# Loading three half batches of q and k in another way: a plain load turned on TensorE, and two transposes from long source rows

## The chip, the cores and the metric
The kernel runs on one core of one Trainium2 chip. The metric is the device time of the whole program in microseconds (us). The core has five instruction streams that run side by side and meet at semaphores: TensorE (PE in the profile, its weight loads as PEld), VectorE (DVE), ScalarE (ACT), GpSimd (POOL) and SyncE (SP, which here only issues DMA transfers). Each engine works through its own list strictly in order.

## The reference
Eight batches, eight heads, 576 tokens, head dimension 64, all in float32. The computation is causal attention with a decay, followed by a feed-forward block with a short convolution and a gate:

```python
scores = scale * np.matmul(q, k.transpose(0, 1, 3, 2))
cum = np.cumsum(np.log(np.clip(f, 0.0001, 1.0)), axis=-1)
scores = np.where(causal, -1e9, scores + cum[:, :, :, None] - cum[:, :, None, :])
attn = softmax(scores)                       # over the last axis
x = (attn @ v), heads side by side           # 8 x 576 x 512
h = np.maximum(x @ w_in, 0.0)                # 512 -> 1024
conv_out[:, s] = sum(conv_w[k] * h[:, s + k - 1] for k in range(3))
out = (h / (1 + np.exp(-conv_out))) @ w_out  # 1024 -> 512
```

## The kernel before, in words
**Half batches.** Attention is done in 16 half batches of four heads (hb 0 to 15). For each, q and k arrive as two tiles of 128 partitions by 2,304 columns (four heads times 576 tokens). A float32 number is read as two 16-bit halves, so the 64 numbers of a token are 128 halves, one for each partition: the upper half of each number is its bfloat16 value and lies on an odd partition, the lower half on an even one. The transfer itself turns tokens into columns (`dma_start_transpose`, line 199). Even partitions are then of no use as numbers. For hb 0 to 5 an operation on VectorE multiplies them by zero and puts constants on three of them (`clamp`, line 205; tasks cl0 to cl5), after which two small transfers from DRAM (`rows_of`, lines 220 and 221; tasks rw1 to rw5) write the decay into some of these rows, so that one matmul gives score plus decay. From hb 6 on, two transfers do all of this (`fill`). hb 0 takes its decay through two additional matmuls and needs no rows from DRAM.

**Tasks.** For one half batch: q and k loads (tasks q*hb*.0 and q*hb*.1, for q and k), cleaning, decay rows, scores on TensorE in six groups (sd: blocks on the diagonal of two heads, so: the other blocks of one head, st: the tail of 64 tokens; line 319, with a mask matmul at line 327), the exponentials on ScalarE (ed, eo, et; lines 360, 377, 339), the product with v (pv, line 395), the division by the row sum on VectorE (n, lines 402 and 403), a turn back on TensorE (t, line 411) and its copy (tx, line 416). The feed-forward part of a batch is eight times f (line 425), r (ScalarE, line 435), c and d (VectorE, lines 440 and 442), a (ScalarE, line 459), g (VectorE, line 463), then o (line 470), its eviction e (line 480) and the store s.

**Order.** Nothing is scheduled by a planner. The string `ORDER` names all tasks in one sequence, and each engine gets its tasks in that sequence. A task that waits therefore holds back all that comes after it on its engine, SyncE's queue of transfers among them. The string begins as follows; the part from `q3.1` on is the second place that the change concerns:

```
cw cl0.0 q2.1 cl2.1 cl0.1 q1.0 cl1.0 q1.1 cl1.1 sd0 ed0 so0.0 eo0.0 ...
f0.4 r0.1 q3.1 d0.0 h0 r0.2 r0.3 cl3.1 c0.2 a0.0 r0.4 c0.3 d0.3 sd4 ... q3.0 eo4.0 a0.3 st2 q5.1 q5.0
f0.5 eo4.1 v1.0 cl3.0 rw3 g0.0 ... so5.1 eo5.1 g0.3 wo0 f0.7 r0.7 cl5.1
cl5.0 rw5 sd7 ed7 ...
```

The four transfers of hb 0 come before this, straight in the code. sd7 is the second pair of heads of hb 3 and is its first score task, so it is the one that meets the wait for rw3; in the same way sd2 is the first of hb 1.

**Storage.** q and k of four half batches lie in a ring of four tiles (qk0 to qk3), so hb 5 uses the tile of hb 1. PSUM is four tiles (ps0 to ps3), handed from task to task in the order of the string. hg0 and hg1 hold the gated values of two batches; hg1 is free until the second batch's feed-forward starts. Before, the rows of the convolution's weights lie in hg1 at the start and two constant rows in hg0.

Of the kernel before, what the change touches and what calls it, by code (L numbers as in the profile page):

```python
# [18 lines left out]
eo1.1 ki@POOL v0.0 v0.1 st0 rw1 v0.2 sd2 so2.0 v0.3 va0.0 cwt so2.1 v0.4 va0.1 et0 sd3 ed2 eo2.1 ed3 so3.0 eo2.0 pv0.0  # L19
n0.0 rw2 pv0.1 eo3.0 n0.1 so3.1 eo3.1 va1.0 va1.1 sd5 ed5 st1 et1 pv0.2 n0.2 wi0 wic0@POOL wi1 wic1@POOL pv1.0 n1.0  # L20
pv1.1 n1.1 pv1.2 n1.2 zc t0 so5.0 tx0@ACT eo5.0 wi3 wi2 wic3@ACT t1 tx1@DVE f0.0 f0.1 f0.2 f0.3 r0.0 wic2@ACT c0.0
f0.4 r0.1 q3.1 d0.0 h0 r0.2 r0.3 cl3.1 c0.2 a0.0 r0.4 c0.3 d0.3 sd4 so4.1 so4.0 ed4 d0.2 q3.0 eo4.0 a0.3 st2 q5.1 q5.0
f0.5 eo4.1 v1.0 cl3.0 rw3 g0.0 f0.6 r0.5 v1.1 a0.2 et2 c0.4 d0.4 v1.2 v1.3 a0.4 so5.1 eo5.1 g0.3 wo0 f0.7 r0.7 cl5.1
cl5.0 rw5 sd7 ed7 c0.1 g0.4 wo1 so7.1 eo7.1 c0.7 sd6 so6.1 eo6.1 g0.2 v1.4 so6.0 r0.6 va3.0 st3 et3 ed6 q4.1 c0.5 d0.5
so7.0 eo7.0 eo6.0 a0.5 c0.6 sd10 ed10 d0.1 q4.0 sd11 ed11 pv3.0 pv3.1 d0.7 va3.1 pv3.2 n3.0 va2.0 n3.1 n3.2 pv2.0
va2.1 wo2 woc0@ACT n2.0 a0.1 pv2.1 n2.1 pv2.2 a0.7 n2.2 so10.1 eo10.1 woc1@POOL v2.0 v2.3 t3 t2 tx2@ACT so10.0 eo10.0
# [43 lines left out]
class Plan:  # L70
# [34 lines left out]
def kernel(  # L105
# [11 lines left out]
    nc = tc.nc  # L117
# [37 lines left out]
    one1 = cpool.tile([128, 1], FP32, name="one1")  # L155
    lim = cpool.tile([128, 4], FP32, name="lim")
    mask = cpool.tile([128, 128], BF16, name="mask")
    taps = cpool.tile([128, NFF, 3, 128], FP16, name="taps")
    lit = cpool.tile([128, 6], FP32, name="lit")
    lii = cpool.tile([128, 3], I32, name="lii")  # L160
    hix = cpool.tile([128, 128], I32, name="hix")
# [20 lines left out]
    ps_t = [psum.tile([128, 1024], FP32, name=f"ps{t}") for t in range(4)]  # L182

    fsb, cum = u_t[0], u_t[1]
    cwrow = hg_t[1].rearrange("p f s -> p (f s)").bitcast(FP32)[0:3, 0:D_FF]

    plan = Plan({"ps": 4, "p": NP, "pt": NPT, "va": NVA, "vf": NVF, "xm": NX, "rc": NRC, "xt": NXT, "ht": NHT, "u": NU,
                 "hg": NHG, "ob": NOB, "pd": NPD, "p3": NP3})
# [3 lines left out]
    def ps_of(name):  # L192
        return ps_t[slot[name, "ps"]]


    def load_qk(hb, h0, nh, side):
        t, src = ((stq_t, q), (stk_t, k))[side]
        t = t[hb % RING]
        nc.sync.dma_start_transpose(  # L199
            t.bitcast(U16)[:, h0 * S:(h0 + nh) * S],  # L200
            src[hb // 2, HH * (hb % 2) + h0:HH * (hb % 2) + h0 + nh].bitcast(U16).rearrange("h s d2 -> (h s) d2"))

    def clamp(hb, h0, nh, side):
        t = (stq_t, stk_t)[side][hb % RING].bitcast(U16)[:, h0 * S:(h0 + nh) * S]
        nc.vector.tensor_scalar(t, t, lim[:, 2 * side:2 * side + 1], lim[:, 2 * side + 1:2 * side + 2],  # L205
                                op0=ALU.mult, op1=ALU.add)
# [52 lines left out]
    for side in range(2):  # L259
        nc.vector.tensor_copy(lim[:, 2 * side:2 * side + 1], lit[:, 1:2])  # L260
    nc.vector.tensor_scalar(sel_k, hfx[:, 0:4], lit[:, 2:3], None, op0=ALU.is_equal)
    nc.vector.tensor_scalar(ident, hfx, lit[:, 0:1], None, op0=ALU.is_equal)
    nc.vector.tensor_scalar(mask, hfx, lit[:, 0:1], -1e30, op0=ALU.is_lt, op1=ALU.mult)
    nc.vector.tensor_scalar(sel_q, hfx[:, 0:4].unsqueeze(2).broadcast_to((128, 4, 128)), lit[:, 0:1], -1.0,
                            op0=ALU.is_equal, op1=ALU.mult)
    nc.vector.tensor_scalar(one3, hfx[0:3, 0:3], lit[0:3, 0:1], None, op0=ALU.is_equal)

    plus, minus = (hg_t[0].bitcast(BF16)[0:BH, x, :] for x in range(2))
    nc.gpsimd.memset(plus, 1.0)
    nc.gpsimd.memset(minus, -1.0)  # L270
    nc.gpsimd.memset(zero, 0.0)
# [156 lines left out]
    def ht_of(b, ff):  # L428
        return ht_t[slot[f"r{b}.{ff}", "ht"]]
# [11 lines left out]
        else:  # L441
            nc.vector.scalar_tensor_tensor(u, ht[:, 2:2 + S], cwt[:, ff, 1:2], u, op0=ALU.mult, op1=ALU.add)  # L442

    def tap_weights(ff):
        for x in range(3):
            nc.gpsimd.tensor_scalar(taps[:, ff, x, :], ident, cw[:, ff, x:x + 1], None, op0=ALU.mult)

    def conv_pe(b, ff):
        ps, ht = ps_of(f"k{b}.{ff}"), ht_of(b, ff)
        for x in range(3):  # L450
            for a in range(2):
                nc.tensor.matmul(ps[:, MB + 288 * a:MB + 288 * (a + 1)], taps[:, ff, x, :],
                                 ht[:, x + 288 * a:x + 288 * (a + 1)], start=(x == 0), stop=(x == 2))

    def tanh(b, ff):
        if (b, ff) in CONV_PE:
            nc.scalar.activation(hg_of(b, ff), ps_of(f"k{b}.{ff}")[:, MB:MB + S], AF.Tanh)
# [62 lines left out]
    for hb in range(NHB):  # L520
        b = hb // 2
        was = hb - RING
        old = [f"st{was}"] + [f"sd{2 * was + y}" for y in range(2)] + [
            f"so{2 * was + y}.{s}" for y in range(2) for s in range(2)] if was >= 0 else []
        if hb == 0:
            for p in range(2):
                add(f"cl0.{p}", "DVE", [], lambda p=p: [clamp(0, 2 * p, 2, side) for side in (1, 0)])
            ready = [["cl0.0"], ["cl0.1"]]
        else:
            for side in range(2):  # L530
                add(f"q{hb}.{side}", "SP", old, lambda hb=hb, side=side: load_qk(hb, 0, 4, side))
            if hb < NCL:
                for side in range(2):
                    add(f"cl{hb}.{side}", "DVE", [f"q{hb}.{side}"], lambda hb=hb, side=side: clamp(hb, 0, 4, side))
                add(f"rw{hb}", "SP", [f"cl{hb}.{side}" for side in range(2)] + ["ki"], lambda hb=hb: rows_of(hb))
                ready = [[f"rw{hb}"]] * 2
            else:
                add(f"fi{hb}", "SP", [f"q{hb}.0", f"q{hb}.1", "zc", "ki"], lambda hb=hb: fill(hb))
                ready = [[f"fi{hb}"]] * 2
        if hb % 2 == 0:  # L540
            for kb in range(NKB):
                add(f"v{b}.{kb}", "SP", [], lambda b=b, kb=kb: load_v(b, kb), take=["vf"] if kb == 0 else [],
                    behind=[f"v{b}.0"] if kb else [])
# [102 lines left out]
```

## Time and profile before
| | |
|---|---|
| two runs | 261.69 and 263.29 us, median 262.49 |
| span of the profiled execution | 262.6 us |
| TensorE busy | 236.1 us, 90% |
| VectorE busy | 213.2 us, 81% |
| ScalarE busy | 207.1 us, 79% |
| GpSimd busy | 64.4 us, 25% |
| cleaning on VectorE, 128x2304 | 10 times, 876 ns each |
| issue of a transposing transfer on SyncE, min / median / max | 1.34 / 2.8 to 3.0 / 5.43 us, 34 in all |

The span is that of one profiled execution; beyond it the runs give only the whole time, and the median lies 0.1 us below the span. The profile names work by engine and source line. An idle time in front of an instruction is put down to what released it: `[2.59 <-DMA qk<-image]` says that the engine stood still for 2.59 us and that a transfer from the decay image into a q/k tile ended the wait. SPq is SyncE's own queue: its rows are the time in which it issued a transfer, not the transfer's own time. The granted clock of TensorE is listed by stretch; 0.50 is half speed.

### The profile page before, as it was taken

The numbers are of one execution on the slowest core, as the hardware profiler recorded it, in microseconds if no ns is written. First come the engines' busy times: TensorE is split into PE (matmuls) and PEld (weight loads), VectorE is DVE, ScalarE is ACT, GpSimd is POOL, SyncE is SP. The second block draws the span as 40 slices with busy tenths as digits, with TensorE's granted clock in tenths as the row PEclk, the third lists the DMA queues.
The fourth block names the chain that finished last, engine by engine and source line by source line (L and its number), as shares of the span: only waits on it lengthen the run. The fifth ranks groups of instructions, "written<-read, shape, count | busy, mean of one in ns | idle before, by whom it ended". The sixth has DMA issues, their size and how long they took to land.

```text
span 262.6 us, 6608 instructions
## 1 busy us (share of the span) xinstructions
PE 236.1 (90%) x2712; PEld 170.2 (65%) x2712; DVE 213.2 (81%) x342; ACT 207.1 (79%) x275; POOL 64.4 (25%) x104
## 2 busy tenths in 40 slices
PE   2495999578869999999999999999999999999991
PEld 1373787357645866778665788579758876766450
DVE  6553166987957999998997979999899999999940
ACT  3163669979887998996798999898999889696732
POOL 8400550014031104017003272027104641100000
PEclk9998599999979999999999999999999999999998
DMA  6999999999799999999999889998999901012225
GB/s 140 210 237 178 273 183 192 205 284 173 191 226 211 210 195 221 228 252 194 205 233 237 218 191 198 286 249 158 219 247 204 300 5 60 25 41 79 82 100 181
DMA packets 123328, 49.37 MB, mean 188 GB/s; under 512 B 113346, under 2 KB 114370, under 8 KB 123298
## 3 DMA queue, kind: packets, MB, share of 16 engines
q1 hardware_dynamic: 122908, 48.07, 86.1%
q0 software_dynamic: 304, 0.73, 1.0%
q8 instruction: 21, 0.34, 0.6%
q10 hardware_dynamic: 86, 0.16, 0.3%
q14 instruction: 9, 0.07, 0.1%
HBM read 19.91 MB, written 10.17 MB: 115 GB/s over the span
## 4 chain that ended last, share of the span: by engine, by line
PE 67%; SPq 10%; DVE 9%; ACT 7%; DMA 3%; issue 2%; ACTq 0%; DVEq 0%
PE ps L425 20%; PE ps L470 18%; PE ps L319 14%; PE ps L395 8%; SPq L199 8%; DMA qk<-image 3%; ACT pp L377 3%; PE ps L474 3%; DVE hg L463 3%; DVE xm L403 2%; PE ps L411 2%; PE ps L327 2%; ACT pp L360 1%; ACT hg L459 1%; DVE u L442 1%
## 5 line engine op out<-in xcount | busy, mean ns | idle before, releaser
L319 PE MATMUL ps<-qk 128*128 128x128 bf16 (+2 forms) x576 | 67.2, 249 | 13.5 <-DMA qk<-image 7.2
L425 PE MATMUL ps<-xt,w_in_f 128*128 128x288 f16 x512 | 69.5, 288 | 1.4 <-ACT xt L416 1.0
L377 ACT ACTIVATE pp<-ps 128x1024 f16<-128x1024 f32 x64 | 64.2, 1028 | 5.2 <-PE ps L319 3.5
L319 PEld LDWEIGHTS <-qk 128*128 128x128 bf16 x576 | 42.9, 102 | 31.9 <-DVE u L440 5.6
L440 DVE SCALAR_TENSOR_TENSOR u<-ht,cwt 128x576 f32<-128x576 f16 x64 | 54.4, 858 | 6.8 <-ACT ht L435 6.8
L425 PEld LDWEIGHTS <-w_in_f 128*128 128x128 f16 x512 | 49.3, 98 | 16.0 <-issue 2.8
L470 PE MATMUL ps<-w_out_f,hg 128*128 128x512 f16 x256 | 59.4, 379 | 0.0
L442 DVE SCALAR_TENSOR_TENSOR u<-ht,cwt,u 128x576 f32<-128x576 f16 x64 | 53.4, 845 | 1.7
L463 DVE SCALAR_TENSOR_TENSOR hg<-hg,ht 128x576 f16<-128x576 f16 x64 | 51.0, 820 | 2.6 <-ACT hg L459 2.6
L459 ACT ACTIVATE hg<-u,cw 128x576 f16<-128x576 f32 x64 | 48.9, 782 | 3.9 <-DVE u L442 3.7
L435 ACT ACTIVATE ht<-ps 128x576 f16<-128x576 f32 x64 | 40.8, 658 | 8.8 <-PE ps L425 7.4
L470 PEld LDWEIGHTS <-hg 128*128 128x128 f16 x256 | 24.4, 98 | 25.4 <-issue 0.4
L395 PE MATMUL ps<-va,pp 128*128 128x65 f16 x896 | 34.2, 193 | 0.8 <-ACT pp L377 0.4
L395 PEld LDWEIGHTS <-pp 128*128 128x128 f16 x896 | 32.5, 98 | 2.0 <-ACT pp L377 0.5
L234 POOL CAST va<-vf 128x1024 f16<-128x1024 f32 x16 | 17.6, 1105 | 63.9 <-DMA vf<-in_v_dram 50.8
L403 DVE TENSOR_TENSOR xm<-ps,rc 128x512 f16<-128x512 f32 (+1 forms) x48 | 28.9, 602 | 1.7
L363 POOL TENSOR_SCALAR_AFFINE_SELECT pp<-pd 128x1024 f16<-128x1024 f32 x16 | 19.6, 1230 | 43.3 <-ACT pd L360 43.3
L360 ACT ACTIVATE pp<-ps 128x1024 f16<-128x1024 f32 x16 | 16.3, 1027 | 15.3 <-PE ps L319 8.8
L480 ACT COPY ob<-ps 128x1024 f32<-128x1024 f32 (+1 forms) x20 | 16.5, 824 | 7.3 <-issue 5.0
L402 DVE RECIPROCAL rc<-ps 128x8 f32<-128x8 f32 (+1 forms) x48 | 9.3, 194 | 11.6 <-PE ps L395 10.6
L205 DVE TENSOR_SCALAR qk<-qk,lim 128x2304 uint16<-128x2304 uint16 (+1 forms) x14 | 10.6, 790 | 9.0 <-DMA qk<-in_k_dram 5.8
L360 ACT ACTIVATE pd<-ps 128x1024 f32<-128x1024 f32 x16 | 16.2, 1029 | 1.6 <-PE ps L319 0.7
(74 smaller groups left out, 170.9 us busy)
## 6 DMA issues: line engine op xcount, KB each, us to landing
vf<-in_v_dram SPq DMA_DIRECT2D x32, 256.0 KB
out_dram<-ob SPq DMA_DIRECT2D x16, 512.0 KB
qk<-blank SPq DMA_DIRECT2D x10, 540.0 KB
ob<-in_moe_w_in_dram SPq DMA_DIRECT2D x4, 512.0 KB
ob<-in_moe_w_out_dram SPq DMA_DIRECT2D x4, 512.0 KB
vf<-in_v_dram SPq DMA_DIRECT2D x8, 128.0 KB
out_dram<-ob SPq DMA_DIRECT2D x16, 64.0 KB
qk<-image SPq DMA_DIRECT2D x10, 36.0 KB
```

The costliest lines, as they stand in the source:

```text
L319: nc.tensor.matmul(o, tk[:, h * S + k0:h * S + k0 + 128], tq[:, h * S + q0:h * S + q0 + n], start=first, stop=last and hb > 0)
L360: nc.scalar.activation(o, ps_of(f"sd{i}").rearrange("p (s c) -> p s c", s=2), AF.Exp, scale=SCALE)
L377: nc.scalar.activation(pair(i)[:, s, 512:1536], ps_of(f"so{i}.{s}"), AF.Exp, scale=SCALE)
L395: nc.tensor.matmul(o, block(hb, h, m, n), va[:, h, m, 0:D + 1], start=(m == 0), stop=(m == n))
L403: nc.vector.tensor_tensor(xm[:, 2 * u:2 * u + nj, :].rearrange("p j (h d) -> p j h d", d=D), got[:, :, :, 0:D], r.unsqueeze(3).broadcast_t ...
L425: nc.tensor.matmul(ps[:, MB + 288 * a:MB + 288 * (a + 1)], w_in_f16[:, cc, 128 * ff:128 * (ff + 1)], xt[:, cc, 288 * a:288 * (a + 1)], sta ...
L435: nc.scalar.activation(ht_of(b, ff)[:, 1:1 + S], ps_of(f"f{b}.{ff}")[:, MB:MB + S], AF.Relu, scale=0.5)
L440: nc.vector.scalar_tensor_tensor(u, ht[:, 0:S], cwt[:, ff, 0:1], ht[:, 1:1 + S], op0=ALU.mult, op1=ALU.add)
L442: nc.vector.scalar_tensor_tensor(u, ht[:, 2:2 + S], cwt[:, ff, 1:2], u, op0=ALU.mult, op1=ALU.add)
L459: nc.scalar.activation(hg_of(b, ff), u_t[slot[f"c{b}.{ff}", "u"]], AF.Tanh, scale=cw[:, ff, 1:2])
L463: nc.vector.scalar_tensor_tensor(hv, hv, 1.0, ht_of(b, ff)[:, 1:1 + S], op0=ALU.add, op1=ALU.mult)
L470: nc.tensor.matmul(ps[:, 512 * (c % 2):512 * (c % 2 + 1)], hg_of(b, ff)[:, 128 * c:128 * (c + 1)], w_out_f16[:, ff, :], **kw)
```

## The change
Three half batches get q and k in another way; the others stay.

- **hb 1.** The two transposing transfers become plain ones (`load_plain`): 18 tokens' worth of float32 per partition into hg1, in pieces of 2,304 bytes. In the place of cl1.0 and cl1.1, `turn_plain` turns each side on TensorE, 18 transposes of 128x128 into one PSUM tile in two batches of nine, both into the same part of the tile. The first nine are read out by VectorE, the second nine by ScalarE; that reading cleans as `clamp` did and puts the tokens back in order, which a plain load deals out over partitions. cl1.0 and cl1.1 take a PSUM tile each.
- **hb 3 and hb 5.** The transfer still transposes, but its source is seen as rows of w tokens, 8 for hb 3 (288 rows of 2 KB) and 144 for hb 5 (16 rows of 36 KB), and it goes into hg1. The result has the tokens in another order, so cleaning reads it with a stride and writes the q/k tile in order: the q side on VectorE, the k side on ScalarE.
- All three use the same room, hg1. So hb 3's transfers wait for hb 1's transposes, and hb 5's wait for hb 3's cleaning, side by side. In the string, cl3.0 therefore moves ahead of q5.0. Nothing else in the string changes: cl1.0 and cl1.1 stay ahead of sd0, and now hold TensorE work.
- The convolution's rows go to hg0, the constant rows to another part of hg0, a second identity matrix in bfloat16 is made at the start, and code that was not in use (`taps`) goes.

```diff
-f0.4 r0.1 q3.1 ... a0.3 st2 q5.1 q5.0
-f0.5 eo4.1 v1.0 cl3.0 rw3 g0.0 f0.6 ...
+f0.4 r0.1 q3.1 ... a0.3 st2 q5.1 cl3.0
+q5.0 f0.5 eo4.1 v1.0 rw3 g0.0 f0.6 ...
...
+    LONG = {3: (8, ("DVE", "ACT")), 5: (144, ("DVE", "ACT"))}
...
+    spare = hg_t[1].rearrange("p f s -> p (f s)")
+
+    def load_long(hb, side, w):
+        src = (q, k)[side][hb // 2, HH * (hb % 2):HH * (hb % 2) + HH].bitcast(U16).rearrange("h s d2 -> (h s) d2")
+        nc.sync.dma_start_transpose(
+            spare.bitcast(U16)[:, HS * side:HS * (side + 1)].rearrange("p (w r) -> p w r", w=w),
+            src.rearrange("(r w) d2 -> r (w d2)", w=w))
+
+    def clamp_long(hb, side, w, e):
+        t = (stq_t, stk_t)[side][hb % RING].bitcast(U16)[:, 0:HS].rearrange("p (r w) -> p r w", w=w)
+        i = spare.bitcast(U16)[:, HS * side:HS * (side + 1)].rearrange("p (w r) -> p r w", w=w)
+        clean(t, i, side, e)
+
+    def clean(t, i, side, e):
+        if e == "ACT":
+            nc.scalar.activation(t, i, AF.Identity, scale=lim[:, 2 * side:2 * side + 1], bias=lim[:, 2 * side + 1:2 * side + 2])
+        else:
+            {"DVE": nc.vector, "POOL": nc.gpsimd}[e].tensor_scalar(
+                t, i, lim[:, 2 * side:2 * side + 1], lim[:, 2 * side + 1:2 * side + 2], op0=ALU.mult, op1=ALU.add)
+
+    def load_plain(hb, side):
+        src = (q, k)[side][hb // 2, HH * (hb % 2):HH * (hb % 2) + HH].rearrange("(i h) s d -> i (h s) d", i=2)
+        nc.sync.dma_start(spare.bitcast(FP32)[:, HS // 2 * side:HS // 2 * (side + 1)].rearrange("p (i x) -> p i x", i=2),
+                          src.rearrange("i (p j) d -> p i (j d)", j=9))
+
+    def turn_plain(hb, side):
+        for p in range(2):
+            o = ps_of(f"cl{hb}.{side}").bitcast(BF16)
+            i = spare.bitcast(BF16)[:, HS * side + p * HS // 2:HS * side + (p + 1) * HS // 2]
+            for j in range(9):
+                nc.tensor.transpose(o[:, 128 * j:128 * (j + 1)], i[:, 128 * j:128 * (j + 1)], ident_b)
+            t = (stq_t, stk_t)[side][hb % RING].bitcast(U16)[:, p * HS // 2:(p + 1) * HS // 2].rearrange("r (t j) -> r t j", j=9)
+            clean(t, o.bitcast(U16)[:, 0:2 * S].rearrange("r (j t) -> r t j", j=9), side, ("DVE", "ACT")[p])
+
     def load_qk(hb, h0, nh, side):
+        if hb == 1:
+            return load_plain(hb, side)
+        if hb in LONG:
+            return load_long(hb, side, LONG[hb][0])
...
     def clamp(hb, h0, nh, side):
+        if hb == 1:
+            return turn_plain(hb, side)
+        if hb in LONG:
+            return clamp_long(hb, side, LONG[hb][0], LONG[hb][1][side])
...
-                    add(f"cl{hb}.{side}", "DVE", [f"q{hb}.{side}"], lambda hb=hb, side=side: clamp(hb, 0, 4, side))
+                    add(f"cl{hb}.{side}", "DVE", [f"q{hb}.{side}"], lambda hb=hb, side=side: clamp(hb, 0, 4, side),
+                        **(dict(take=["ps"], give=[("ps", f"cl{hb}.{side}")]) if hb == 1 else {}))
```

More of the change, by code (lines that the diff above doesn't have):

```diff
@@ L21 @@
 pv1.1 n1.1 pv1.2 n1.2 zc t0 so5.0 tx0@ACT eo5.0 wi3 wi2 wic3@ACT t1 tx1@DVE f0.0 f0.1 f0.2 f0.3 r0.0 wic2@ACT c0.0
-f0.4 r0.1 q3.1 d0.0 h0 r0.2 r0.3 cl3.1 c0.2 a0.0 r0.4 c0.3 d0.3 sd4 so4.1 so4.0 ed4 d0.2 q3.0 eo4.0 a0.3 st2 q5.1 q5.0
-f0.5 eo4.1 v1.0 cl3.0 rw3 g0.0 f0.6 r0.5 v1.1 a0.2 et2 c0.4 d0.4 v1.2 v1.3 a0.4 so5.1 eo5.1 g0.3 wo0 f0.7 r0.7 cl5.1
+f0.4 r0.1 q3.1 d0.0 h0 r0.2 r0.3 cl3.1 c0.2 a0.0 r0.4 c0.3 d0.3 sd4 so4.1 so4.0 ed4 d0.2 q3.0 eo4.0 a0.3 st2 q5.1 cl3.0
+q5.0 f0.5 eo4.1 v1.0 rw3 g0.0 f0.6 r0.5 v1.1 a0.2 et2 c0.4 d0.4 v1.2 v1.3 a0.4 so5.1 eo5.1 g0.3 wo0 f0.7 r0.7 cl5.1
 cl5.0 rw5 sd7 ed7 c0.1 g0.4 wo1 so7.1 eo7.1 c0.7 sd6 so6.1 eo6.1 g0.2 v1.4 so6.0 r0.6 va3.0 st3 et3 ed6 q4.1 c0.5 d0.5
@@ L147 @@
     ident = cpool.tile([128, 128], FP16, name="ident")
+    ident_b = cpool.tile([128, 128], BF16, name="ident_b")
     one3 = cpool.tile([3, 3], FP32, name="one3")
@@ L157 @@
     mask = cpool.tile([128, 128], BF16, name="mask")
-    taps = cpool.tile([128, NFF, 3, 128], FP16, name="taps")
     lit = cpool.tile([128, 6], FP32, name="lit")
@@ L184 @@
     fsb, cum = u_t[0], u_t[1]
-    cwrow = hg_t[1].rearrange("p f s -> p (f s)").bitcast(FP32)[0:3, 0:D_FF]
+    cwrow = hg_t[0].rearrange("p f s -> p (f s)").bitcast(FP32)[0:3, 0:D_FF]
     plan = Plan({"ps": 4, "p": NP, "pt": NPT, "va": NVA, "vf": NVF, "xm": NX, "rc": NRC, "xt": NXT, "ht": NHT, "u": NU,
@@ L261 @@
     nc.vector.tensor_scalar(sel_k, hfx[:, 0:4], lit[:, 2:3], None, op0=ALU.is_equal)
+    nc.vector.tensor_scalar(ident_b, hfx, lit[:, 0:1], None, op0=ALU.is_equal)
     nc.vector.tensor_scalar(ident, hfx, lit[:, 0:1], None, op0=ALU.is_equal)
@@ L266 @@
     nc.vector.tensor_scalar(one3, hfx[0:3, 0:3], lit[0:3, 0:1], None, op0=ALU.is_equal)
-    plus, minus = (hg_t[0].bitcast(BF16)[0:BH, x, :] for x in range(2))
+    plus, minus = (hg_t[0].bitcast(BF16)[0:BH, 6 + x, :] for x in range(2))
     nc.gpsimd.memset(plus, 1.0)
@@ L442, in conv @@
             nc.vector.scalar_tensor_tensor(u, ht[:, 2:2 + S], cwt[:, ff, 1:2], u, op0=ALU.mult, op1=ALU.add)
[L444 to L453, printed above, removed]
     def tanh(b, ff):
```

## The prediction, made before the result was known
> **What bounds the kernel now.** I read the page's chain of work that ended last, then the timeline of SyncE's queue and of the engines from 0 to 60 us, then the busy times by stretch. The chain first:
>
> ```profile
> PE 67%; SPq 10%; DVE 9%; ACT 7%; DMA 3%; issue 2%; ACTq 0%; DVEq 0%
> ```
>
> Two thirds of the end are TensorE's own work, and SyncE's queue is next. The busy times by stretch say where TensorE is not the bound (columns: stretch in us, length, then PE, PEld, DVE, ACT, POOL busy, granted clock of TensorE, DMA share, GB/s):
>
> ```profile
> 0.00:10.00 10.00, 1.52 (x9) 1.13 (x10) 7.79 (x23) 3.25 (x3) 8.09 (x38) 1.00 0.77 156
> 10.00:22.50 12.50, 12.17 (x113) 9.08 (x112) 3.90 (x6) 6.21 (x7) 0.44 (x1) 1.00 1.20 214
> 22.50:25.60 3.10, 0.16 (x2) 0.07 (x2) 1.94 (x8) 0.33 (x1) 0.00 (x0) 0.86 1.05 192
> 25.60:31.00 5.40, 5.40 (x31) 3.55 (x32) 0.00 (x0) 2.60 (x3) 2.59 (x4) 0.50 0.98 242
> 45.60:53.30 7.70, 4.31 (x35) 2.83 (x34) 7.59 (x11) 6.49 (x10) 0.00 (x0) 1.00 1.06 203
> 140.00:200.00 60.00, 60.00 (x731) 43.27 (x729) 53.79 (x82) 56.58 (x76) 19.68 (x22) 1.00 1.01 220
> ```
>
> TensorE starts late (10 us), works through hb 0 until 22.5, stands for 3 us, runs at half clock until 31, and stands again before 53.3. From about 83 us on it is full (60.00 of 60.00 from 140 to 200). So the end is the time at which TensorE gets its early work done: an early us lost is lost unless one of the early waits takes it up. Those waits, in the timelines:
>
> ```profile
> 25.56 0.59 PE L319 MATMUL ps<-qk 128*128 128x128 bf16 x4 [2.94 <-DMA qk<-image]
> 53.27 0.38 PE L319 MATMUL ps<-qk 128*128 128x128 bf16 x4 [2.59 <-DMA qk<-image]
> 74.97 0.38 PE L319 MATMUL ps<-qk 128*128 128x128 bf16 x4 [1.70 <-DMA qk<-image]
> ```
>
> They are the decay rows of hb 1, hb 3 and hb 4 (rw1, rw3, rw4), and the change works on what leads to the first two. SyncE's queue shows why they are late (start, length):
>
> ```profile
> 11.23 2.57 SPq L199 DMA_TRANSPOSE qk<-in_q_dram  x1
> 13.84 2.72 SPq L199 DMA_TRANSPOSE qk<-in_k_dram  x1
> 16.61 2.53 SPq L199 DMA_TRANSPOSE qk<-in_q_dram  x1
> ...
> 32.78 4.98 SPq L199 DMA_TRANSPOSE qk<-in_k_dram  x1
> 37.81 4.78 SPq L199 DMA_TRANSPOSE qk<-in_q_dram  x1
> 42.69 3.36 SPq L199 DMA_TRANSPOSE qk<-in_k_dram  x1
> 46.09 2.87 SPq L199 DMA_TRANSPOSE qk<-in_q_dram  x1
> 49.01 0.58 SPq L227 DMA_DIRECT2D vf<-in_v_dram  x1
> 49.69 0.38 SPq L220 DMA_DIRECT2D qk<-image  x1
> ```
>
> Rows 1 and 2 are hb 1, rows 4 to 7 are hb 3 and hb 5, and the last is rw3, issued only when hb 5's two transfers have been issued. That queue order stays.
>
> **hb 1: what is removed.** Two transposing issues (2.57 and 2.72 us) and two cleanings (0.876 us each). A plain load of 576 KB is not in the trace; the nearest rows are the 512 KB weight loads, which landed at 31.30 and 32.66, so 1.36 us x 576/512 = 1.53 us; the other bound is what the transposing ones took, 2.1 and 2.45 us between landings (14.34, 16.45, 18.90). I take 1.53: q lands at 14.34 + 1.53 = 15.9, k at 17.4.
>
> **hb 1: what is added.** 36 transposes on TensorE, and, in the listing of the changed kernel by engine, all 36 stand ahead of sd0. TensorE takes its list in order, so **the whole of hb 0, which started at 9.85 us, now waits for hb 1's data**. Also the second nine of each side write the part of PSUM that the first nine wrote, so TensorE waits for VectorE's reading in between. Matmuls of 128 columns stand 0.107 us apart at 10 to 13 us and 0.056 apart from 16 us on; I take 0.107 x 9 = 0.96 for nine. Cleaning 1,152 elements with a stride on VectorE: its row 128x512 takes 0.691 us and 128x256 0.424 (line 403), so 1.05 ns an element and 0.15 fixed: 1.36 us; bounds 0.57 (row 128x1152 of line 205) and 1.36. ScalarE copies 128x1152 in 1.127. From the last transpose to the next engine I take 0.2 us (line 411 and the copy behind it).
>
> The sum: q 15.9 + 0.96 + 0.2 + 1.36 + 0.05 + 0.96 = 19.4; k 0.96 + 0.2 + 1.36 + 0.05 + 0.96 makes 23.0, when sd0 starts. With the quick ends (0.5 for nine, 0.76 for the reading, as the 128x1152 copy of line 416 on VectorE) it is 20.0. ScalarE ends k's cleaning at 23.0 + 0.2 + 1.13 = 24.3, and rw1 can be issued there instead of at 21.5. From sd0 to the end of hb 0 it was 22.25 - 9.85 = 12.4 us, of which 4.4 at the wide spacing. So hb 1 starts at 35.4 instead of 25.56: 9.8 late. The 2.94 us wait on rw1 is thereby used up (rw1 lands near 28), and hb 1 no longer runs at half clock, which gives back half of 5.5 us. **TensorE is 7.1 us late by the end of hb 1**; with the quick ends (20.0, and hb 0 in 10.2) 1.9.
>
> The Trainium skill (TensorE: Matmul & The Clock Gate, Part 4) says that transposes do not count as TensorE being busy for the clock, so hb 0 would again begin at half clock after them, as in my sum; if they did count, 2.2 us of it would go. In this trace the transposes of line 411 lie between matmuls, so no row decides it.
>
> **hb 3 and hb 5.** The transfers' cost from long rows is not in the trace. Lower bound: the plain rate, 1.53 us; upper bound: the longest transposing issue, 5.43. I take hb 5's own rows, 3.36 and 2.87, as the bytes are the same, and keep the bounds. The Trainium skill (DMA: Bandwidth & Descriptors, Latency and other measured facts) gives 350 to 400 GB/s for contiguous transposes and 261 for others; this trace's 2.57 us for 590 KB is 229. By the higher rate (1.6 us) sd7 would come 1.3 us earlier than below.
>
> Cleaning loses its dense reading: 0.15 + 2304 x 1.05 ns = 2.57 us on VectorE (bounds 0.876 and 2.57), and on ScalarE, by 128x576 in 0.658 and 128x1152 in 1.127, 2.3 at most, I take 2.05 (128x1024 in 1.028 doubled). **The new wait**: hb 5 loads into the room that hb 3's cleaning reads, so q5.1 waits for cl3.1 on ScalarE and q5.0 for cl3.0 on VectorE, and behind them on SyncE's queue wait v1.0, rw3 and all later loads.
>
> ScalarE reaches cl3.1 after its three line 435 pieces (43.5 before), so 43.5 + 7.1 = 50.6, and is done at 52.6; hb 3's own landing (43.1 and about 46 before, some 3 us later now, as SyncE is held 2.9 us by rw1) is earlier, so its load is covered unless it takes 4 us more. q5.1 is issued from 52.6 to 56.0. VectorE reaches cl3.0 at 46.98 - 0.88 (cl3.1 is gone from it) + 7.1 = 53.2 and ends at 55.8. q5.0: 56.0 + 2.87 = 58.9; v1.0 0.6; rw3 from 59.5, and from its issue to TensorE's matmul it took 53.27 - 49.69 = 3.58. **sd7 at 63.1 instead of 53.27: 9.8 late.** TensorE without that wait would be there at 50.7 + 7.1 = 57.8, so the 2.59 us wait becomes 5.3.
>
> What lies beside it: ScalarE's second long cleaning (cl5.1) falls into that wait; the first adds 2 us to ScalarE, which was 7.00 of 7.00 busy from 38.6 to 45.6, and is covered by the same wait; without it, 2 us. hb 5's cleaning on VectorE ends at 58.9 + 2.65 (issue to landing of hb 1's q: 13.80 to 16.45) + 2.57 = 64.1, rw5 lands by 67.5, where sd10 comes at 58.0 + 9.8. Idle pieces of 0.77 and 1.14 us on VectorE take up what cl5.0 adds there. The second identity (0.29 us, line 262) and the moved constants lie before the first data. From here on everything, SyncE's loads included, is shifted alike, and I see no wait behind it that gets shorter.
>
> Sum against the execution's 262.6 (0.1 above the median of the runs): **262.6 + 9.8 = 272.4, predicted 272**. All quick ends together: 1.9 late, cl3.0 done at 48.9, q5.0 issued by 50.5, sd7 at 54.7, so +1.4: 264. Both long transfers at 5.43: sd7 at 67.7, so +14.4: 277.
>
> **Rivals.**
> - *The delay is mostly absorbed.* hb 0 runs faster than I think and hb 5's transfers and cleaning come at their low ends: 264 to 267.7. For it: 12 us of early idle and half clock. Against: the queue order with its new waits. Chance 0.20, time 265.5.
> - *Faster.* The plain load and the long rows free the transfers so much that all three waits on the decay image (7.2 us) vanish: 255.4. It decides only if sd0 starts within the 3 us that TensorE stands before hb 1, so by 13 us; yet q2.1 alone lands at 14.34, and the turns come after. Chance 0.07.
> - *Long rows are far slower.* If 16 rows of 36 KB are still moved in short packets (the page counts 113,346 of 123,328 packets under 512 bytes), these now come from places 36 KB apart; at twice the longest issue (10.9 us each) sd7 comes at 79: +25, 288. No row speaks for it, none excludes it. Chance 0.10.
> - *The change does not do what it says*, the long rows moving just like the short ones: that is my sum already.
>
> **How the numbers follow.** Forecast (267.7 to 277) 0.63, the rivals 0.20, 0.07 and 0.10. The range takes in the low end and a little of the slow rival: 264 to 280. Two per cent (5.2 us), about what a measurement of this kernel can tell from no change, puts the bounds at 257.2 and 267.7: faster 0.06, same 0.21, slower 0.73.
>
> **What would show it.** Right: sd0 (the first line 319 matmul) at 21 to 23 us behind transposes in four groups; no wait on the decay image before hb 1; SyncE standing before hb 5's transfers until VectorE has cleaned hb 3; sd7 near 63 with a wait of about 5 us. Wrong: sd0 before 18, or rw3 issued before 53, or hb 5's transfers of over 6 us.

## The result and the profile after

The changed kernel is slower: **276.09 us** (275.50 and 276.68 in two runs) against 262.49, a ratio of 1.055 with a 95% interval of 1.038 to 1.073. The prediction was 272.0 with a range of 264 to 280. By these medians the kernel takes 13.6 us more, where 9.8 were forecast. The profiled execution took 275.5 us; its span is 273.8, and before it was 262.6, so 11.2 us more by span. Wherever the record has both, an execution's time is 1.7 to 1.8 us above its span. The ratios leave out disturbed executions of either kernel, and in the last four experiments this leaves only two of seven executions of the kernel before (261.28 and 265.03 us, the others up to 269.31).

The chain of work that ended last, on the page of the changed kernel:

```profile
PE 58%; ACT 17%; DVE 10%; SPq 6%; DMA 4%; issue 3%; ACTq 0%; DVEq 0%
```

TensorE's share fell from 67% to 58%, and ScalarE's rose from 7% to 17%: a new engine stands on the path, which the prediction had beside it.

Busy times by stretch, changed kernel (stretch, length, then PE, PEld, DVE, ACT, POOL, granted clock, DMA share, GB/s):

```profile
10.00:23.20 13.20, 4.51 (x37) 3.96 (x38) 6.05 (x10) 1.44 (x2) 0.00 (x0) 1.00 0.96 227
...
51.70:63.50 11.80, 5.70 (x36) 3.57 (x34) 8.28 (x8) 11.80 (x14) 0.00 (x0) 0.86 0.55 129
140.00:200.00 60.00, 59.89 (x713) 43.87 (x708) 54.60 (x82) 56.21 (x77) 18.54 (x20) 1.00 1.03 215
```

Two stretches hold the loss. From 10 to 23.2 TensorE works 4.51 us of 13.2, and that is the turning of hb 1. From 51.7 to 63.5 it works 5.70 of 11.8 while ScalarE is busy for all 11.80, and the transfers run at about half their usual share. From 140 to 200 TensorE is full again, as before.

TensorE's timeline, changed kernel (start, length, operation, idle time before it and what ended it):

```profile
15.55 1.14 PE L227 MATMUL ps<-ident_b,hg 128*128 128x128 bf16 x9 [10.12 <-DMA hg<-in_q_dram]
18.27 2.08 PE L227 MATMUL ps<-ident_b,hg 128*128 128x128 bf16 x18 [1.57 <-DVE qk L214]
21.91 1.12 PE L227 MATMUL ps<-ident_b,hg 128*128 128x128 bf16 x9 [1.57 <-DVE qk L214]
...
23.25 0.31 PE L363 MATMUL ps<-qk 128*128 128x128 bf16 x1
...
55.28 0.37 PE L371 MATMUL ps<-mask,ident 128*128 128x256 bf16 x1 [3.43 <-ACT ht L479]
...
63.53 0.40 PE L363 MATMUL ps<-qk 128*128 128x128 bf16 x4 [2.38 <-DMA qk<-image]
67.65 0.60 PE L363 MATMUL ps<-qk 128*128 128x64 bf16 x4 [1.98 <-ACT pp L404]
```

The first three rows are the 36 transposes, with VectorE's reading in between (1.57 us each time). Row 4 is sd0's first product, at 23.25 instead of 10.33 (its weight load was at 9.85). The 2.94 us wait on hb 1's rows is gone. The last three rows hold 7.8 us of idle time, where before had one wait, the 2.59 us at sd7; the two that end with ScalarE are new.

These waits have a second price, the clock. The trace lists a granted clock of 0.50 from 55.3 to 58.7 and from 68.9 to 72.4 us, soon behind the first and the third wait, with 3.1 and 3.3 us of TensorE's work in these stretches. By an estimate from these numbers, half of that work time, 1.5 us each, is lost to the clock; the first 1.5 us only shorten the wait at sd7. Before had such stretches as well, from 24.7 to 31.6 behind the wait on hb 1's rows and from 75.9 to 79.4 behind the one at 74.97. What ScalarE and VectorE were doing at these waits, in their timelines:

```profile
49.70 4.31 ACT L212 ACTIVATE qk<-hg,lim 128x2304 uint16<-128x2304 uint16 x1
...
62.04 4.65 ACT L212 ACTIVATE qk<-hg,lim 128x2304 uint16<-128x2304 uint16 x1
66.52 1.08 ACT L404 ACTIVATE pp<-ps 128x1024 f16<-128x1024 f32 x1
```

```profile
52.92 2.21 DVE L214 TENSOR_SCALAR qk<-hg,lim 128x2304 uint16<-128x2304 uint16 x1
61.63 2.35 DVE L214 TENSOR_SCALAR qk<-hg,lim 128x2304 uint16<-128x2304 uint16 x1 [3.13 <-DMA hg<-in_q_dram]
```

ScalarE cleans the k sides of hb 3 and hb 5 in 4.31 and 4.65 us; the exponential that TensorE waits for at 67.65 stands right behind the second. SyncE's queue, and one line of its list of waits (total, times, longest):

```profile
34.96 4.57 SPq L201 DMA_TRANSPOSE hg<-in_k_dram  x1
39.59 4.62 SPq L201 DMA_TRANSPOSE hg<-in_q_dram  x1
54.04 2.78 SPq L201 DMA_TRANSPOSE hg<-in_k_dram  x1
56.93 2.86 SPq L201 DMA_TRANSPOSE hg<-in_q_dram  x1
...
60.47 0.42 SPq L263 DMA_DIRECT2D qk<-image  x1
```

```profile
SPq L201 <- ACT pp L404: 11.5, 1, 11.5
```

By this list hb 5's transfers wait 11.5 us for ScalarE (the timeline has 9.8 us between the end of one issue, 44.21, and the next), until hb 3's cleaning is done at 54.0, and rw3 (the last row) stands behind them. The releaser is given as line 404, but the event falls on the end of the cleaning at line 212 (49.70 + 4.31).

### The profile page after: what moved, and what is told of

Same layout as the page of the kernel before. It is cut to its first block, busy times and chain, and to the rows that moved or that the text cites. A ratio compares the mean times of both kernels' runs of the same rounds, so it can differ in the third digit from the quotient of the medians.

```text
span 273.8 us, 6688 instructions
## 1 busy us (share of the span) xinstructions
PE 237.5 (87%) x2748; PEld 172.1 (63%) x2748; DVE 218.8 (80%) x341; ACT 217.9 (80%) x279; POOL 64.8 (24%) x104
## 2 busy tenths in 40 slices
DMA packets 114624, 49.37 MB, mean 180 GB/s; under 512 B 104098, under 2 KB 105122, under 8 KB 114562
## 4 chain that ended last, share of the span: by engine, by line
PE 58%; ACT 17%; DVE 10%; SPq 6%; DMA 4%; issue 3%; ACTq 0%; DVEq 0%
PE ps L503 16%; PE ps L469 14%; PE ps L363 10%; PE ps L439 6%; ACT pp L421 6%; SPq L238 5%; DVE hg L496 4%; ACT qk L212 3%; DMA qk<-blank 3%; PE ps L507 3%; PE ps L455 2%; ACT pp L404 2%; DVE u L486 2%; DMA hg<-in_q_dram 2%; ACT hg L492 2%
## 5 line engine op out<-in xcount | busy, mean ns | idle before, releaser
L363 PE MATMUL ps<-qk 128*128 128x128 bf16 (+2 forms) x576 | 64.7, 243 | 6.7 <-DMA qk<-image 2.4
L484 DVE SCALAR_TENSOR_TENSOR u<-ht,cwt 128x576 f32<-128x576 f16 x64 | 55.6, 876 | 5.3 <-ACT ht L479 5.2
L363 PEld LDWEIGHTS <-qk 128*128 128x128 bf16 x576 | 41.9, 99 | 27.0 <-issue 9.3
L492 ACT ACTIVATE hg<-u,cw 128x576 f16<-128x576 f32 x64 | 49.2, 785 | 6.2 <-DVE u L486 5.9
L496 DVE SCALAR_TENSOR_TENSOR hg<-hg,ht 128x576 f16<-128x576 f16 x64 | 53.1, 854 | 1.0 <-ACT hg L492 1.0
L371 PE MATMUL ps<-mask,ident 128*128 128x512 bf16 (+1 forms) x40 | 15.2, 382 | 3.7 <-ACT ht L479 3.4
```

Of the source, the lines that this page charges most:

```text
L363: nc.tensor.matmul(o, tk[:, h * S + k0:h * S + k0 + 128], tq[:, h * S + q0:h * S + q0 + n], start=first, stop=last and hb > 0)
L484: nc.vector.scalar_tensor_tensor(u, ht[:, 0:S], cwt[:, ff, 0:1], ht[:, 1:1 + S], op0=ALU.mult, op1=ALU.add)
L492: nc.scalar.activation(hg_of(b, ff), u_t[slot[f"c{b}.{ff}", "u"]], AF.Tanh, scale=cw[:, ff, 1:2])
L496: nc.vector.scalar_tensor_tensor(hv, hv, 1.0, ht_of(b, ff)[:, 1:1 + S], op0=ALU.add, op1=ALU.mult)
```

## Experiments

The twelve runs split the change. For each I give the time, its ratio to the kernel before on the same chip, and the span. Single kernels vary: the kernel before had spans from 262.2 to 266.2 us beside the first four of them alone. So I also use **lateness**: the start of the same ScalarE instruction (cleanings left out of the count) in one trace minus its start in the trace of before. It tells at which point of the program time is lost. Each row is a single execution; that of "neither part" took 265.75 us, where the kernel's ten ran from 261.52 to 267.73. Columns: the instruction's start before, in us.

| kernel | 38.5 | 49.2 | 57.7 | 81.3 | 94.3 | 179.9 | 210.3 | 257.2 |
|---|---|---|---|---|---|---|---|---|
| full change | 6.3 | 9.8 | 12.6 | 8.7 | 9.6 | 9.2 | 10.9 | 11.2 |
| full change again | 7.9 | 11.5 | 14.1 | 10.5 | 11.8 | 12.1 | 13.6 | 14.2 |
| neither part | -0.1 | 0.3 | 1.5 | -2.4 | -1.1 | -1.1 | 1.1 | 1.4 |
| turn only | 8.3 | 8.0 | 6.2 | 2.6 | 3.7 | 3.5 | 5.9 | 6.2 |
| turn only, late | -0.1 | 1.8 | 3.1 | -0.8 | 1.1 | 1.5 | 3.7 | 4.0 |
| full, turned late | 1.3 | 7.1 | 11.0 | 7.1 | 8.4 | 8.8 | 10.3 | 10.7 |
| long rows only (hb 3, hb 5) | 0.5 | 4.0 | 7.0 | 4.0 | 4.5 | 5.7 | 7.8 | 8.1 |
| hb 3 long alone | 0.0 | 3.6 | 1.9 | -1.2 | 0.3 | 0.7 | 2.8 | 3.1 |
| hb 5 long alone | 0.4 | 0.1 | 3.0 | -0.9 | 0.6 | 0.6 | 3.2 | 3.5 |
| full, short rows | 7.0 | 8.5 | 10.8 | 6.9 | 10.4 | 9.9 | 11.5 | 12.2 |
| turn and hb 3 long | 7.1 | 10.7 | 8.8 | 5.9 | 7.5 | 8.8 | 9.4 | 9.7 |
| turn and hb 3 short | 7.7 | 9.3 | 7.4 | 4.5 | 8.1 | 7.3 | 9.5 | 9.8 |
| full, VectorE cleans | 8.2 | 10.6 | 13.8 | 9.9 | 11.8 | 11.5 | 12.6 | 13.3 |

**Turn only.** hb 3 and hb 5 as before, with the order of before.

```diff
-    LONG = {3: (8, ("DVE", "ACT")), 5: (144, ("DVE", "ACT"))}
+    LONG = {}
```

> Half batch 1 loaded plainly and turned on TensorE, half batches 3 and 5 loaded and cleaned as before; the order string of before. Theory (two delays, one behind the other: the turns ahead of sd0, and the waits and slow cleanings of half batches 3 and 5): sd0 at about 22.8 us as in the changed kernel, TensorE some 6 us late by the end of half batch 1, of which the wait on rw3 (2.6 us before) takes up about 1.8; sd7 near 57.7 instead of 53.3, span about 267 (265 to 269). Rival (the start is the whole loss): span 273 to 275. Rival (the start is absorbed by the early waits): 262 to 264.

Measured: 270.57 us, 1.018 (1.011 to 1.026), span 268.8, inside the theory's 265 to 269. It is 8.3 us late at the end of hb 1 (some 6 were expected), and the wait on hb 3's rows, which before is 2.59, takes up 2.1 of it by 57.7. The rest stays.

**Long rows only.** hb 1 as before.

```diff
-        if hb == 1:
-            return load_plain(hb, side)
...
-        if hb == 1:
-            return turn_plain(hb, side)
```

> Half batches 3 and 5 from long source rows with cleaning out of the shared room, half batch 1 as before. Theory: sd0 at 9.9 us and half batch 1 as before; ScalarE's first long cleaning takes about 4.3 us, hb 5's transfers wait for it, sd7 near 57.5 instead of 53.3, the second cleaning stands ahead of ed7 and costs another 2.5; span about 269 (267 to 271), so that this loss and the one of the turns alone add up to the whole. Rival (the start is the whole loss): span 262 to 264.

Measured: 272.88 us, 1.029 (1.021 to 1.038), span 270.8, at the upper end of the theory's span of 267 to 271. TensorE's timeline of this kernel:

```profile
49.47 0.37 PE L367 MATMUL ps<-mask,ident 128*128 128x256 bf16 x1 [3.43 <-ACT ht L475]
...
57.88 0.40 PE L359 MATMUL ps<-qk 128*128 128x128 bf16 x4 [1.54 <-DMA qk<-image]
62.26 0.60 PE L359 MATMUL ps<-qk 128*128 128x64 bf16 x4 [2.23 <-ACT pp L400]
```

It is the same triple as in the full change (3.43, 2.38, 1.98): first cleaning, rows of hb 3 behind the queue's wait (here 6.7 us), second cleaning. So the two waits behind the cleanings belong to the long rows, whatever happens to hb 1; the one between them stands in the kernel before as well (2.59).

**Full change, hb 1 turned later.** The first side behind hb 0's first scores, the second behind its second pair.

```diff
-... q1.0 cl1.0 q1.1 cl1.1 sd0 ed0 so0.0 eo0.0 so0.1 eo0.1 q2.0 cl2.0 sd1 ed1 so1.0 ...
+... q1.0 q1.1 sd0 ed0 so0.0 eo0.0 so0.1 eo0.1 cl1.0 q2.0 sd1 ed1 cl1.1 cl2.0 so1.0 ...
```

> The full change, but in the order string cl1.0 stands behind half batch 0's first three score groups and cl1.1 behind its fourth. Theory: sd0 back at 9.9 us, half batch 1 begins near 28.5 instead of 34.0 (the turns now cost TensorE their own time and two waits on VectorE), the waits of half batch 5 remain; sd7 near 58.5, span about 268.5 (266 to 271). Rival (the position of the turns does not matter since the wait for hb 3's cleaning ends last): span 273 to 275.

Measured: 274.20 us, 1.033 (1.025 to 1.040), span 273.3. The theory missed: the span is 2.3 us over its 266 to 271 and in the rival's range. hb 1 is only 1.3 us late, but 11.0 us are lost by 57.7. TensorE's timeline of this kernel shows where:

```profile
52.55 0.37 PE L371 MATMUL ps<-mask,ident 128*128 128x256 bf16 x1 [5.71 <-ACT ht L479]
...
60.13 0.40 PE L363 MATMUL ps<-qk 128*128 128x128 bf16 x4 [0.34 <-DMA qk<-image]
65.70 1.93 PE L363 MATMUL ps<-qk 128*128 128x64 bf16 x8 [3.42 <-ACT pp L404]
```

SyncE, held by rw1 until 26.1 us, issued hb 3's transfers no earlier than in the full change (36.35 and 41.68 against 34.96 and 39.59). ScalarE then stood 2.19 us for their landing and cleaned behind that, so TensorE waits 5.71 instead of 3.43. With the long rows, then, most of what an earlier start wins is lost again at hb 3's cleaning.

**Full change, short rows.** The way through hg1, both engines and all waits stay; the rows have the plain length, so the cleaning reads without a stride.

```diff
-    LONG = {3: (8, ("DVE", "ACT")), 5: (144, ("DVE", "ACT"))}
+    LONG = {3: (1, ("DVE", "ACT")), 5: (1, ("DVE", "ACT"))}
```

> The full change, but half batches 3 and 5 transposed from rows of one token (w = 1) into the shared room, so that cleaning reads without a stride; waits and engines as in the full change. Theory (the stride makes ScalarE's cleaning slow): ScalarE's two cleanings take 2.1 to 2.3 us instead of 4.3 and 4.6, VectorE's 0.9 instead of 2.2, sd7 near 61.2, span about 269 (267 to 271); the transfers themselves are issued in 2.8 to 5 us as before. Rival (16-bit data from SBUF is slow on ScalarE whatever the stride): 4.3 us again, span 273 to 275. Rival (long source rows speed the transfers and their absence costs): later transfers, span over 275.

Measured: 277.21 us, 1.043 (1.035 to 1.052), span 274.8. Cleaning takes 2.30 and 2.37 us on ScalarE and 0.87 and 0.88 on VectorE, so the stride itself costs ScalarE 2.0 and 2.3 us, as the theory had it, and the transfers are issued as fast as before. The time does not follow; the span is 3.8 us over the theory's 267 to 271:

```profile
53.97 0.27 PE L371 MATMUL ps<-mask,ident 128*128 128x256 bf16 x1 [1.41 <-ACT ht L479]
...
62.46 0.40 PE L363 MATMUL ps<-qk 128*128 128x128 bf16 x4 [3.19 <-DMA qk<-image]
...
99.77 0.38 PE L363 MATMUL ps<-qk 128*128 128x128 bf16 x4 [2.08 <-DMA qk<-image]
```

The first wait falls from 3.43 to 1.41, the wait on hb 3's rows grows from 2.38 to 3.19, the one behind the second cleaning falls from 1.98 to 0.67, and what is won by 81.3 (1.9 us) is lost at 99.77, on the rows of a later half batch.

**Turn and hb 3 long; hb 5 as before.** hb 5 goes into its own tile, so it does not wait for hb 3's cleaning.

```diff
-    LONG = {3: (8, ("DVE", "ACT")), 5: (144, ("DVE", "ACT"))}
+    LONG = {3: (8, ("DVE", "ACT"))}
```

> Half batch 5 is loaded and cleaned as before (a transposing load into its own tile, dense VectorE cleaning); half batch 3 keeps its long rows, half batch 1 its turns. Theory (the queue's wait for half batch 3's cleaning, and the second ScalarE cleaning, which delays the exps by 4 us, are what the long rows cost beside the first cleaning): the wait of 11.5 us on the queue goes, half batch 3's rows are issued near 56 instead of 60.9, the wait at 63.5 shrinks from 2.4 to under 1, and the time is 270 (267 to 272). Rival (the first ScalarE cleaning alone holds TensorE through 55, and what is behind it follows from that): 274 to 276.

Measured: 274.19 us, 1.029 (1.023 to 1.035), span 272.3. The steps came as expected: no wait of hb 5's transfers on a cleaning, hb 3's rows issued at 56.03, no wait of sd7 on them. They win 3.8 us by 57.7, but only 1.5 (against the first execution of the full change) to 4.5 (against the second) at the end; TensorE stands 1.49 us at 98.21 on a later half batch's fill. The first ScalarE cleaning still holds TensorE, 3.44 us at 56.15. The steps on the queue are the theory's, the time is the rival's (274 to 276).

**Full change, both sides cleaned on VectorE.**

```diff
-    LONG = {3: (8, ("DVE", "ACT")), 5: (144, ("DVE", "ACT"))}
+    LONG = {3: (8, ("DVE", "DVE")), 5: (144, ("DVE", "DVE"))}
```

> The full change with both cleanings of the long rows on VectorE; ScalarE cleans nothing. Theory (ScalarE's two cleanings of 4.3 and 4.65 us hold its gelu and exps, and through them TensorE): VectorE spends 4.5 us more in all, ScalarE 9 less, the idle 3.4 at 55.3 and 2.0 at 67.7 on TensorE go, the queue's wait ends some 5 us earlier: 270 (267 to 273). Rival (VectorE, as loaded here as ScalarE, passes the same loss on through the relus and convolutions): 275 to 277.

Measured: 277.20 us, 1.041 (1.037 to 1.046), span 275.9. The rival holds. VectorE's and TensorE's timelines of this kernel:

```profile
50.97 2.25 DVE L214 TENSOR_SCALAR qk<-hg,lim 128x2304 uint16<-128x2304 uint16 x1
56.24 2.21 DVE L214 TENSOR_SCALAR qk<-hg,lim 128x2304 uint16<-128x2304 uint16 x1
```

```profile
65.67 0.59 PE L363 MATMUL ps<-qk 128*128 128x128 bf16 x4 [4.40 <-DMA qk<-image]
```

The cleanings are half as long as on ScalarE and begin no earlier, because they stand behind VectorE's convolutions; the second ends at 58.4, q5.0 is issued then, and the row write behind it lets sd7 start at 65.67. So moving the cleanings to the other engine wins nothing here; where they stand in that engine's list, and what the queue puts behind them, explains the waits that are left.

**Turn only, late.** The two edits above together: no long rows, order of the third experiment at the start.

> No long rows, the order of before, but half batch 1's turns behind the score products of half batch 0 (first side) and behind the second pair's (second side). Theory (turning costs by delaying the first score product; behind it the 36 transposes cost TensorE at most some 2 us at full clock): 3 to 5 us under the turn-only kernel's 270.6, so 267 (265 to 268.5), still not under before. Rival (the transposes' place does not matter, since what follows waits for the same transfers and row writes): 270 to 271.

Measured: 267.87 us, 1.008 (1.005 to 1.012), span 266.6. Without long rows the place of the turns is worth 2.7 us (270.57 to 267.87; 2.2 by span), and its ratio is the lowest of all versions that keep a part of the change (hb 3 or hb 5 long alone, below, come close, with shorter spans and wider intervals). Nine transposes take 0.66 us here, where the clock is up, and 1.14 at the start of the full change; VectorE's reading still holds TensorE 1.64 us in front of a second nine.

**Neither part.** Loads, cleanings and order of before in the changed file.

> Loads, cleanings and order of before in the changed file: only the second identity, the moved constants and the smaller set of tiles remain of the change. Theory (those do nothing): 264.6, within 1 us of before. Rival (the 2 to 2.7 us that every variant so far loses at 203 to 226 comes from these common parts): 266.5 to 267.5.

Measured: 265.55 us, 0.999 (0.990 to 1.008), span 264.0. The second identity and the moved constants cost nothing that shows within this interval. The trace also has two swings of the table that all variants share, without the change's loads: the gain of 2.9 to 3.9 us between 57.7 and 81.3 (before has a 1.70 us wait at 74.97 and half clock behind it) and the loss of 0.6 to 2.6 between 180 and 210. So neither swing is the change's doing. Whether they belong to the one execution of before that was profiled, or to the parts that all versions of the changed file share, stays open with the one trace of before. With this row subtracted, the full change is 11.2 us late at 57.7 and 81.3, and 9.8 at the end.

**Full change again.**

> The full change once more, beside the parts. Theory (the kernel before had 262.5 in its two runs of the first comparison but 264.6 and 265.7 in the medians of the later ones; the change costs some 10 us): 275 to 276.5 where before has 265.5, a ratio near 1.04, at the lower end of the interval first found (1.038 to 1.073). Rival (the ratio of 1.055 holds): 279 to 281.

Measured: 278.23 us, 1.059 (1.040 to 1.077), span 276.8; the ratio is the rival's, and the time lies between the two ranges, since the kernel before lay between 261.28 and 269.31 us on this chip. This execution is 3 us longer than the first; 1.7 of it is there by 38.5. sd0 comes 0.6 later (23.86 against 23.25), and the timelines of TensorE in hb 0 show the rest. First execution:

```profile
24.77 0.22 PE L363 MATMUL ps<-qk 128*128 128x128 bf16 x1
24.82 0.22 PE L366 MATMUL ps<-sel_k,kc 128*128 128x128 bf16 x1
```

Second:

```profile
25.56 0.31 PE L363 MATMUL ps<-qk 128*128 128x128 bf16 x1
25.67 0.31 PE L366 MATMUL ps<-sel_k,kc 128*128 128x128 bf16 x1
```

In the first, matmuls follow each other by 0.056 us from 24.5 on, 1.3 us after sd0 began. In the second they are still 0.107 apart at 25.67, and stay at the wide spacing until 27.4, 3.5 us after sd0. How soon TensorE speeds up differs between executions of one kernel.

**hb 3 long alone, hb 5 long alone.** From the second experiment (hb 1 as before), one of the two entries left: the first `+` line for the one kernel, the second for the other.

```diff
-    LONG = {3: (8, ("DVE", "ACT")), 5: (144, ("DVE", "ACT"))}
+    LONG = {3: (8, ("DVE", "ACT"))}
+    LONG = {5: (144, ("DVE", "ACT"))}
```

> Only half batch 3 comes from long rows; half batches 1 and 5 as before. Theory (of the 6.7 us that the two long loads cost without the turns, half batch 3 costs the greater part, by ScalarE's cleaning of 4.3 us ahead of its gelus and exps, as the time with half batch 5 restored under the turns says: 3.5 us over the turn-only kernel): 269 to 270 where before has 265.5. Rival (the two cost only together, through the queue's wait of half batch 5's loads for half batch 3's cleaning): under 267.

> Only half batch 5 comes from long rows; with half batch 3 as before the spare room is free when its loads are due, so the queue doesn't wait for a cleaning. Theory (what is left is ScalarE's one cleaning of 4.6 us and VectorE's longer one): 267 to 269 where before has 265.5. Rival (half batch 5's cost does not hang on the wait): 270 or more, so that the two parts add up to more than 272.9.

Measured: 268.48 us, 1.019 (1.006 to 1.033), span 265.7, and 267.75 us, 1.019 (1.004 to 1.033), span 266.2. TensorE's timeline with hb 3 alone, then with hb 5 alone:

```profile
49.03 0.27 PE L367 MATMUL ps<-mask,ident 128*128 128x256 bf16 x1 [3.43 <-ACT ht L475]
```

```profile
52.47 0.38 PE L359 MATMUL ps<-qk 128*128 128x128 bf16 x4 [1.68 <-DMA qk<-image]
57.98 0.60 PE L359 MATMUL ps<-qk 128*128 128x64 bf16 x4 [3.37 <-ACT pp L400]
```

With hb 3 alone the first cleaning costs TensorE its 3.43 us, but then sd7 needs no wait at all, and before it had one of 2.59: 3.6 us late at 49.2 is 1.9 at 57.7. With hb 5 alone the second cleaning costs 3.37 us and nothing takes it up. With both, the queue issues rw3 at 54.74 instead of 49.64 (hb 3 alone), since hb 5's transfers ahead of it wait for hb 3's cleaning; so sd7 waits 1.54 us on top of the first cleaning's 3.43.

By span the two cost 1.7 and 2.2 us over the kernel with neither part, together 3.9; both at once cost 6.8. In these traces 2.9 us between exist only when both are there, as does the queue's wait. But two executions of one kernel differ by 3.0 us, and the ratios (1.019 and 1.019 alone, 1.029 with both) don't show the 2.9. So the additional wait is shown, its price is not. hb 3 doesn't show as the greater part, as I had it; hb 5's alone came as expected.

**Turn and hb 3 through hg1 with short rows.** No stride, no wait of hb 5 is left.

```diff
-    LONG = {3: (8, ("DVE", "ACT")), 5: (144, ("DVE", "ACT"))}
+    LONG = {3: (1, ("DVE", "ACT"))}
```

> Half batch 1 turned, half batch 3 through the spare room with rows of the plain length and dense cleaning on the same two engines, half batch 5 as before: neither the wait of half batch 5's loads nor the stride is left of the long rows. Theory (wait and stride are all that the long rows cost): turn-only's time and 1 us for ScalarE's 2.3 us of cleaning, 270.5 to 272 where before has 265.5. Rival (what costs is that the cleaning stands behind the gelus on ScalarE at all, whatever its length): 273 to 275, as with the long rows of half batch 3.

Measured: 273.92 us, 1.040 (1.021 to 1.059), span 272.4, the same as with long rows (274.19, 272.3). The time is the rival's: that the stride adds anything to it does not show. ScalarE's cleaning starts at 51.12, lasts 2.31 and holds TensorE 1.42 us at 54.69; by 57.7 it is 1.4 us better than with the stride, and it loses 2.06 at 97.43 on a later half batch's rows. A wait of this kind, on the rows or the fill of a later half batch, stands near this place in all thirteen traces of the changed file, though. It is 1.21 us with neither part (at 89.60), 0.68 in the first execution of the full change (100.24) and 1.05 in the second (102.48), so it is not tied to what was won before 81. What sets it in each kernel no run took apart; this stays open.

## Why the prediction was right

**Right, with its numbers.** hb 0 behind hb 1's data: sd0 at 23.25, forecast 23.0, behind four groups of nine. No wait on the decay image before hb 1. Cleaning on VectorE 2.21 and 2.35 (2.57) and from PSUM 1.48 (1.36). The queue: q5.1 at 54.0 (52.6), rw3 at 60.5 (59.5), sd7 at 63.53 (63.1). hb 5's transfers 2.78 and 2.86 (3.36 and 2.87 taken). The sum to sd7 was 9.8 and measured 10.3. What SyncE stood for was ScalarE's cleaning of hb 3, as in the sum, and not VectorE's, as in the list of signs.

**ScalarE's cleaning was the mis-sized term.** It was taken as 2.05 us from a dense 128x1024 row of PSUM doubled; it is 4.31 and 4.65. It starts 0.9 us earlier than forecast (49.70, forecast 50.6) and ends at 54.0 instead of 52.6. That sd7 came within 0.5 us even so is in part luck: the early start, transfers that were issued 0.6 us quicker, and 3.06 us instead of 3.58 from rw3 to TensorE took back most of the 2.3 us.

**"Covered by the same wait" and "falls into that wait" failed.** The first cleaning holds TensorE 3.43 us *before* it reaches sd7, since the line 479 piece behind it frees the part of PSUM that TensorE's next scores take. So the wait at sd7 shrank to 2.38 where about 5 was forecast: the same gap, opened earlier by another engine. The second cleaning did not fit: it ended at 66.69, sd7's exponential started at 66.52, and TensorE stood another 1.98. That is the 2.4 us (12.6 late at 57.7 against 10.3 at sd7) that the sum to sd7 had no term for, though the kernel with neither part is itself 1.5 late at 57.7.

**The base of the sum.** 9.8 us were added to a span of 262.6 and the result was taken for a time. A time is 1.7 us above its span, so 1.7 of the 3.7 us between the sum (272.4) and the measured 276.09 are this, 1.4 are the change's cost by span (11.2 against 9.8), and 0.6 the distance of the profiled execution from the median.

**The clock in hb 0** was taken at the wide spacing for 4.4 us. It was 1.3 in the first execution (hb 1 at 34.0, forecast 35.4; 6.3 us late, forecast 7.1) and 3.5 in the second (7.9 late): the forecast lies between. That hb 1 no longer runs at half clock held, but the half clock came back behind the new waits (55.3 to 58.7, 68.9 to 72.4), for which the sum had no term. The Trainium skill (TensorE: Matmul & The Clock Gate, Part 4) says that transposes do not count as TensorE being busy for the clock. In all seven traces with the turns ahead, the first score products are still 0.107 us apart behind 36 transposes, which fits. But in two of them the wide spacing ends 1.3 us after sd0's first product, and the seven traces that begin with score products need 3.5 to 4.8 us, which does not fit. So these runs don't decide it.

**"No wait behind it that gets shorter"** seemed to fail, by 3.9 us between 57.7 and 81.3, with 2.0 lost again after 180. The kernel with neither part does the same (3.9 and 2.5), so these are not the change's loads.

**The rivals.** Absorbed and faster: neither was seen; where hb 0 did start early (the third experiment), hb 3's cleaning took most of the gain. Long rows far slower: the issues took 4.57 and 4.62 us for hb 3 (4.98 and 4.78 before) and 2.78 and 2.86 for hb 5. The packets fell from 123,328 to 114,624: 4,128 of these 8,704 fall to hb 1's plain load (turn only has 119,200), 4,576 to hb 5's rows of 36 KB (hb 5 alone has 118,752), and none to hb 3's rows of 2 KB (hb 3 alone has 123,329). Yet neither kind of long row sped up the transfers in any way that shows: alone, hb 3's issues are 4.99 and 4.66 and hb 5's 3.41 and 2.94, where the kernel before has 4.98, 4.78, 3.36 and 2.87. The Trainium skill (DMA: Bandwidth & Descriptors, Latency and other measured facts) gives 350 to 400 GB/s for contiguous transposes. That does not show here: 589,824 bytes in an issue of 2.86 us would be 206, and in the shortest issue of a whole transposing load in any trace, 1.96 us with short rows, 301. In the prediction's own sum, transfers of 1.6 us would bring sd7 1.5 us earlier and not 1.3, since q5.0 could start at 55.8.

**What remains of the cost.** Turning ahead of hb 0 costs 4.8 us by span over neither part, the long rows 6.8, both 9.8 (first execution) to 12.8 (second), all from single executions. No part of the change made the kernel faster, and no version tried beats the kernel before.

## What to carry to other kernels

When a step is moved into an in-order list, cost it at its place: what stands behind it on that engine, and whom that feeds, decides more than its own length. A wait that is to hide a new operation can hide it only if the operation lies inside the wait; one that comes before it merely opens the same gap earlier. And two edits that share a buffer are to be priced together: here the second's transfers had to wait for the first's reader, a wait that neither has alone. A long wait also has a price behind it where the clock falls to 0.50, unless the next wait takes that up.

## What the runs showed of the hardware

- ScalarE reads 16-bit elements from the on-chip buffer with a stride at half its dense pace: 128x2304 in 4.31 us (elements 576 bytes apart) and 4.58 to 4.65 (32 bytes apart), 2.30 to 2.37 without a stride. VectorE's dense pace falls further, from 0.87 to 2.21 (576 bytes apart) and 2.36 (32), but it stays twice as fast as ScalarE.
- Source rows of 2 KB and of 36 KB made a transposing transfer no quicker to issue than rows of 256 bytes (4.99 and 4.66 against 4.98 and 4.78 us; 3.41 and 2.94 against 3.36 and 2.87). Rows of 2 KB left the number of packets as it was (123,329 and 123,328).
- TensorE's first score products stand 0.107 us apart, and how long until they follow each other at half the distance differs: 3.5 to 4.8 us in the seven traces that begin with them, 1.3 to 4.5 in the seven with 36 transposes ahead, 1.3 and 3.5 in two executions of one kernel. The granted clock is listed as 1.00 all this time.
- At or soon behind TensorE's longer waits the listed clock was 0.50 for about 3.4 us (55.3 to 58.7 and 68.9 to 72.4 in the full change) or twice that (24.7 to 31.6 before).
- The same kernel's profiled executions differed by 3.0 us in span (273.8 and 276.8), so a single pair of traces can't carry a difference of that size without the waits in them.
